# Kernel rows in two-bank PSUM tiles, and one exponent fewer: a change to an S4 layer's forward and backward pass

## The chip, the cores and the metric

The kernel runs on one core of a Trainium2 chip. The metric is the device time of one execution in microseconds, from start to end; lower is better. Each core has a matrix engine (PE, with its weight loads shown apart as PEld), a vector engine (DVE), a scalar engine (ACT), a general engine (POOL) and a queue engine (SP) that issues most DMA transfers. Each engine works through its own instruction stream in order and waits on semaphores for the others. Matrix products are written to PSUM, which has eight banks of 512 fp32 columns in each of 128 partitions; only DVE and ACT can copy them out to SBUF, the working memory.

## The reference

The computation is one layer, forward and backward. The forward part, cut to what matters:

```python
xn = _layernorm(x)                                   # x: [1, 2048, 512]
dt = exp(log_dt)[:, None]
P  = exp((dt * (A_re + 1j*A_im))[:, :, None] * arange(L)[None, None, :])   # [512, 128, 2048]
K  = einsum("dn,dnl,dn->dl", Cc, P, dt * Bc).real    # convolution kernel, 512 x 2048
s  = irfft(rfft(xn, padded) * rfft(K, padded))[:L] + xn * Dskip
g  = silu(silu(xn @ w1) @ w2)
out = x + s * g
```

The kernel returns `out` and the gradients of a scalar product with `grad_out` with respect to x, A, B, C (real and imaginary parts), log_dt, Dskip, w1 and w2. The sequence has L = 2048 rows, 512 channels, 128 states per channel, and a feed-forward width of 1792.

## The kernel before

**Kernel rows.** The powers of exp(dt*A) are never formed for all 2048 exponents. Exponent l is split into a sum of an exponent of a table E and one of a table Y. `E_EXP` has 21 entries (256 to 2048 in steps of 256, 0 to 7, and five sums of these), and `Y_EXP` has ten (8 to 56 in steps of 8, and 64, 128, 192). The 512 channels are worked in four blocks `b` of 128, each in two halves `h` of 64. For each half

- `gen_magnitudes` has written, in setup, the magnitudes exp(Re * e) of all 31 exponents (one ACT exponential each, L516) to the DRAM tensor `Md`;
- `gen_phases` (stream P) forms the phases, 16 and then 15 exponents at a time: a DVE product (L572), a DVE shift (L575) and an ACT sine (L579);
- `gen_powers` (stream Q) loads the half's magnitudes (L593) into a part of the tile `ds`, multiplies phase by magnitude on DVE (L607) into E, Y and H, stores E (`Ed`, L609), forms the remaining Y by six DVE products (L618 to L622), and stores Y (`Yd`, L624). E and the magnitudes have one buffer, so the load of the next half waits for the last power product of the half before, and it stands on SP's queue behind the store of Yd;
- `gen_kernel_rows` (stream R) multiplies E by C*B into W (two DVE products for eight channel groups, L642), then forms the kernel rows by PE: for each channel group `q` four matmuls of 84 columns accumulate (L648). Four groups fill a tile `ps_k` of 336 columns, which is copied to `ds` (the part called Xr) in another order of its axes. The tile's tag `pt` has one buffer of one bank. After both halves, rows are selected and summed from Xr by `put` (L660, `ps_e`, `ps_f`) and go by DMA to `Kb` in time order.

**Convolutions.** `gen_conv_x` (X), `gen_conv_fwd` (C) and, in the backward pass, `gen_conv_bwd_fwd` (D) and `gen_conv_bwd` (B) do Fourier transforms by matmuls. Every step fills a PSUM tile of tag `pc` (two buffers of two banks) and copies it to SBUF (1024 columns, or 2048 of bf16). **Feed-forward**: J turns rows, F is the forward product (tag `pf`, three buffers of one bank), and later come A, x, d, w, v, t for its gradients. N, Y, V, T, S, Z give the gradients of A, B, C and dt; `gen_ssm_fold` (N) sums kernel gradients per exponent of E.

**Order.** All engines run under a manual schedule. Each stream is a Python generator that issues a few instructions between two `yield`s. `PLAN` is a string of seven parts with one character per step, and `play` takes one step of the stream named by each. Part 0 is setup, part 1 the kernel rows and forward convolutions, part 2 the gate, part 3 the backward convolutions and feed-forward, parts 4 to 6 the parameter gradients. So PLAN alone sets each engine's and each queue's order. `SLOTS` names, allocation by allocation, which buffer of a tag is taken. `WAYS` has one string per stream: letter by letter, whether its next PSUM copy is made by ACT (`A`, L114) or DVE (`D`, L115).

The functions that the change touches are printed here with the line numbers of the profile.

## Time and profile before

| | us |
|---|---|
| median of 3 runs | 576.76 |
| the three runs | 576.76, 574.21, 577.73 |
| profiled execution, its own time | 574.64 |
| span from first to last instruction in it | 572.9 |
| mean granted TensorE clock | 0.987 of full speed |

The profiled execution is 2.1 us below the median; 1.7 us of its time lie outside the span. The page of the profile gives each engine's busy time as a share of the span, groups of instructions (line, engine, operation, output and input, shapes, count, busy us, mean ns of one, the idle time of the engine before them and who ended it), and the queues of DMA. A view by stretches gives busy time for windows of the span. A releaser is the instruction whose semaphore ended a wait. A busy PE isn't a PE at its peak, since matmuls are pipelined. The span starts at the first instruction, and each stage of PLAN follows the one before with some overlap: setup to about 42 us, rows and forward convolutions to about 206, the gate to about 245, the backward convolutions to about 366, and parameter and weight gradients to the end.

### The profile page before, as it was taken

How to read it: one execution, taken by the hardware profiler on the slowest of the kernel's cores; microseconds unless marked ns; L12 is line 12 of the kernel's file. 1: busy time of each engine (PE TensorE's matmuls, PEld its weight loads, DVE VectorE, ACT ScalarE, POOL GpSimd, SP SyncE). 2: the span in 40 equal slices, each digit the busy share in tenths (PEclk: the TensorE clock that was granted, in tenths of full speed). 3: DMA queues.
4: the chain of work that ended last, by engine and by line, in shares of the span. 5: the costliest groups of instructions: out<-in, count | busy, mean ns of one | idle time of the engine just before them, and what ended most of it. 6: DMA issues, size and time to landing. Idle time of an engine off the chain costs nothing.

```text
span 572.9 us, 14534 instructions
## 1 busy us (share of the span) xinstructions
PE 526.5 (92%) x6008; PEld 394.0 (69%) x6008; DVE 524.7 (92%) x818; ACT 448.1 (78%) x559; POOL 78.3 (14%) x164
## 2 busy tenths in 40 slices
PE   0589998999998999999999999999999999999993
PEld 0346776586767676876677766777678797776772
DVE  7999989999999779999998899969999999993994
ACT  6989998999999859998998977573575786662662
POOL 4251102010100011000010000000000030332221
PEclk9799998999999999999999999999999999999998
DMA  8978798899979989878989789898999998998982
GB/s 229 310 298 229 206 289 255 294 265 244 336 230 252 318 269 345 273 265 242 355 240 287 236 264 295 228 216 159 297 229 208 244 275 212 217 239 261 174 223 101
DMA packets 156644, 144.75 MB, mean 253 GB/s; under 512 B 83489, under 2 KB 132897, under 8 KB 153505
## 3 DMA queue, kind: packets, MB, share of 16 engines
q1 hardware_dynamic: 146816, 121.00, 78.7%
q0 software_dynamic: 6640, 19.67, 10.1%
q10 hardware_dynamic: 3120, 3.15, 1.8%
q8 instruction: 47, 0.77, 0.6%
q14 instruction: 21, 0.16, 0.1%
HBM read 62.91 MB, written 59.38 MB: 213 GB/s over the span
## 4 chain that ended last, share of the span: by engine, by line
PE 38%; DVE 31%; issue 10%; DMA 8%; ACT 6%; POOL 3%; SPq 2%; ACTq 0%; POOLq 0%; DVEq 0%
PE ps_da L1165 7%; PE ps_dx L1189 6%; PE ps_i L449 4%; PE ps_i L462 3%; DMA ds<-Md 3%; PE ps_o L777 3%; PE pt_t L136 2%; PE ps_s L432 2%; DVE Tq L1034 2%; DVE ds L607 2%; PE ps_w L1228 2%; DVE Tp L1034 2%; PE ps_s L404 2%; DMA out_dram<-gout 2%; DVE Tp L1038 2%
## 5 line engine op out<-in xcount | busy, mean ns | idle before, releaser
L114 ACT CAST dA<-ps_s 128x1024 bf16<-128x1024 f32 x86 | 86.6, 1035 | 7.5 <-PE ps_s L404 5.2
L760 PE MATMUL ps_h<-XT,W 128*128 128x256 bf16 x448 | 59.5, 283 | 11.0 <-ACT hT L114 6.6
L114 ACT CAST Vb<-ps_v 128x672 bf16<-128x672 f32 x55 | 39.1, 734 | 28.0 <-PE ps_v L1017 24.5
L760 PEld LDWEIGHTS <-W 128*128 128x128 bf16 x448 | 43.8, 102 | 19.7 <-issue 12.1
L1165 PE MATMUL ps_da<-doT,W 128*128 128x256 bf16 x448 | 56.9, 273 | 0.0
L1257 PE MATMUL ps_w<-dh_tok,xn 128*128 128x256 bf16 x448 | 52.4, 273 | 0.0
L777 PE MATMUL ps_o<-W,aT 128*128 128x512 bf16 x224 | 51.2, 379 | 0.2
L1189 PE MATMUL ps_dx<-W,dhT 128*128 128x512 bf16 x224 | 50.9, 379 | 0.0
L1228 PE MATMUL ps_w<-YD,a_tok 128*128 128x512 bf16 x224 | 50.6, 379 | 0.0
L114 ACT CAST dB<-ps_i 128x1024 bf16<-128x1024 f32 x42 | 41.9, 1031 | 10.6 <-PE ps_i L449 10.4
L1257 PEld LDWEIGHTS <-xn 128*128 128x128 bf16 x448 | 43.0, 98 | 5.7 <-issue 0.4
L1165 PEld LDWEIGHTS <-W 128*128 128x128 bf16 x448 | 41.2, 98 | 6.9 <-issue 1.2
L1168 DVE TENSOR_TENSOR dhT<-ps_da,dhT 128x512 bf16<-128x512 f32 x56 | 37.5, 685 | 7.0 <-PE ps_da L1165 6.7
L777 PEld LDWEIGHTS <-aT 128*128 128x128 bf16 x224 | 21.1, 98 | 25.1 <-ACT aT L768 1.2
L1189 PEld LDWEIGHTS <-dhT 128*128 128x128 bf16 x224 | 21.2, 98 | 24.8 <-issue 1.6
L1228 PEld LDWEIGHTS <-a_tok 128*128 128x128 bf16 x224 | 21.6, 98 | 23.2 <-ACT a_tok L1219 0.2
L114 ACT CAST o<-ps_w 128x256 bf16<-128x256 f32 (+1 forms) x37 | 16.2, 442 | 21.4 <-PE ps_w L1257 10.3
L579 ACT ACTIVATE sn<-V 128x2048 bf16<-128x2048 int16 (+1 forms) x16 | 30.2, 1890 | 0.9 <-DVE ds L607 0.5
L1219 ACT ACTIVATE a_tok<-pt_t 128x1024 bf16<-128x1024 bf16 x28 | 28.7, 1039 | 2.2 <-PE pt_t L136 2.1
L477 DVE TENSOR_TENSOR sp_in<-sp_in,dA 128x2048 bf16<-128x2048 bf16 x24 | 29.3, 1223 | 0.6
L475 DVE TENSOR_TENSOR cm<-sp_in,dA 128x2048 bf16<-128x2048 bf16 x24 | 29.3, 1220 | 0.7
L449 PE MATMUL ps_i<-I,sp_in 64*128 64x128 bf16 x768 | 27.6, 217 | 2.1 <-ACT dB L114 1.1
(240 smaller groups left out, 1244.6 us busy)
## 6 DMA issues: line engine op xcount, KB each, us to landing
Yd<-YD SPq DMA_DIRECT2D x8, 1024.0 KB, 5.2
sp_in<-Ud SPq DMA_DIRECT2D x8, 1024.0 KB, 8.2
h_in<-Hd SPq DMA_DIRECT2D x14, 512.0 KB, 5.1
Ed<-ds SPq DMA_DIRECT2D x8, 672.0 KB, 6.3
Eb<-Ed SPq DMA_DIRECT2D x8, 672.0 KB, 5.6
Hd<-hT POOLq DMA_DIRECT2D x8, 512.0 KB, 7.2
Ud<-dA SPq DMA_DIRECT2D x8, 512.0 KB, 7.2
KXd<-dA SPq DMA_DIRECT2D x4, 1024.0 KB, 5.3
```

Source lines behind the costliest of these rows:

```text
L114: return self.nc.scalar.copy(out=out, in_=in_)
L449: nc.tensor.matmul(out=ps[:, z, g], lhsT=Y[zs, c, g0 + g, :], rhs=k.I2[zs, c].rearrange("p c m -> p (c m)"), start=(c == 0), stop=(c == 1))
L475: TT(out=t2[:], in0=b[:, :, gs], in1=a[:, 1:2, gs].to_broadcast([P, 2, n, P]), op=ALU.mult)
L477: TT(out=b[:, :, gs], in0=b[:, :, gs], in1=a[:, 0:1, gs].to_broadcast([P, 2, n, P]), op=ALU.mult)
L579: nc.scalar.activation(out=sn[:, 0:n], in_=low, func=ACT.Sin, scale=-2 * PI_LO / 2.0 ** PB)
L760: nc.tensor.matmul(out=ps[:, j], lhsT=k.W1[:, dk, ft * P:ft * P + P], rhs=XTv[:, :, dk, :], start=(dk == 0), stop=(dk == DK - 1))
L777: nc.tensor.matmul(out=ps[:], lhsT=aT[:, ft, t * P:t * P + P], rhs=k.W2[:, ft, :], start=(ft == 0), stop=(ft == FT - 1))
L1165: nc.tensor.matmul(out=ps[:, j], lhsT=k.W2[:, ft, dk * P:dk * P + P], rhs=dTv[:, :, dk, :], start=(dk == 0), stop=(dk == DK - 1))
L1168: nc.vector.tensor_tensor(out=dh[:, i0:i0 + 2, :], in0=ps[:], in1=dh[:, i0:i0 + 2, :], op=ALU.mult)
L1189: nc.tensor.matmul(out=ps[:], lhsT=dhs[ft // 8][:, ft % 8, t * P:t * P + P], rhs=k.W1[:, :, ft * P:ft * P + P], start=(ft == 0), stop=(ft ...
L1228: nc.tensor.matmul(out=ps[:], lhsT=at[:, t, :], rhs=k.do[:, t, :], start=(t == 0), stop=(t == k.T - 1))
L1257: nc.tensor.matmul(out=ps[:], lhsT=k.xn[:, t, dk * P:dk * P + P], rhs=dh[:, t].rearrange("p j n -> p (j n)"), start=(t == 0), stop=(t == k ...
```

## The change

- **Two-bank tiles for the rows.** `ps_k` moves from tag `pt` (one buffer, one bank) to tag `pc` (two buffers, two banks, shared with the transforms), has eight channel groups of 128 columns each, of which 84 are used, and is copied once for eight groups: 16 copies of 672 columns instead of 32 of 336. The 32 matmuls are issued in two steps of 16 before the copy.
- **Exponent zero once.** The exponent 0 is put first in `E_EXP`, and phases, magnitudes and power products run over the 30 others (`X_EXP`). Its power, 1 + 0i, is written once into E by two memsets in `gen_first_powers`. Phases come 15 and 15 at a time instead of 16 and 15, and `Md` has 30 entries. E's entries are numbered anew, and the later users of the rows and the fold follow.
- **Order, slots and ways are made anew** for the whole kernel, in all seven parts of PLAN.

```diff
 PLAN = """
-221p32551512p5566073777171165553766767777J767774J6376777pF6767703076767884p6J7677777707F6067FJF86F46673F5F743FF776646FF6
...
+221325p5325515566767571677777766647701JJ70p7775076F6377766F76pF774770J786877J3F773177F06p6676643643F86853376F174F76FFFF6
...
-WAYS = """J=DAADADAA;
-F=AAADAAAAADADDAAAADADAAAAAAAAAAAAAAAAAAAAAAADADDAAAAAAAAADDDADAAADADDDAAA;
+WAYS = """J=DDADADAA;
+F=ADAAAAAAADDAAADAAADAAAAAAAAAAADAAAAAAAAAAAAADDAAAAADAADADDDAAADADDDAAAA;
...
-R=AAAAAAAAAAAAAAAAAAADAADDDAADAAAAAADAADAAAAAAAAAA;
-C=DDDAAAAAAAAAAAAAAAAADDAAAAAAAADAAAAAADAADAADDAADADADDDADAAAAAAAA;
+R=AAAAAAAAAAADAADAAADAAADAAAAAAAAA;
+C=ADDADAAAAAAAAAAAAAAADDAAAAAAAADDAAAAADAAAAADADAAADADDDADAAAAAAAA;
...
-D=AAAADDAAAAAAAAADAAAAAADAAADAAAAAAADAADA;
-d=DDAADAAA;
-B=AAAAAAAAAAAAAADAAAAAAAAAAAAAAAAAAAAAAADAAADAAADAAAAAAAADADA;
-x=AADAAAADADAA;
-V=DAADADDADAAAADAADDAAAAAAAAAAAAAAAAADAAAAAAAAAAAAAAAAAAAAAAAAAAAA;
-Y=AADDDAAA;
-w=AADAAAAAAADAAA;
-v=DAADAAAAAAADAAAAAAAAAAAAAAAA"""
+D=AAAADDAAAAAAAAADAADAAAAAAAAAADAADAAAAAA;
+d=DDADDAAD;
+B=AAAAAAAAAAADAADAADAAAAAAAAAAAAAADAADAAAADAADADAAAAAAAADAA;
+x=AADAADADDADA;
+V=DAAADAAAAAAAAAAAAADADAAADAAAAAAAAAAAAAAAAAAAAAAAAAAAAAAAAAAAAAAA;
+Y=DAAAAAAA;
+w=DADADDAAAAAAAA;
+v=AAADAADAAAADADAAAAAAAAAAAAAA"""
...
-E_EXP = [256 * i for i in range(1, 9)] + list(range(8)) + [258, 260, 262, 516, 772]
+E_EXP = list(range(8)) + [256 * i for i in range(1, 9)] + [258, 260, 262, 516, 772]
 Y_EXP = [8 * j for j in range(1, 8)] + [64, 128, 192]
 NE = len(E_EXP)
+X_EXP = E_EXP[1:] + Y_EXP
+NX = len(X_EXP)
...
-    for i, e in enumerate(E_EXP + Y_EXP):
+    for i, e in enumerate(X_EXP):
         nc.scalar.activation(out=mag[:, :, i], in_=lamr[:].rearrange("p (b d) -> p b d", b=8), func=ACT.Exp, scale=float(e))
...
     for Y in k.Y:
         k.nc.vector.memset(Y[:, 0, :, 0, :], 1.0)
         k.nc.vector.memset(Y[:, 1, :, 0, :], 0.0)
+    E = k.ds[:].rearrange("p t d -> p (t d)")[:, 0:2688].rearrange("p (c q e a) -> p c q e a", c=2, q=16, a=4)
+    k.nc.vector.memset(E[:, 0, :, 0, :], 1.0)
+    k.nc.vector.memset(E[:, 1, :, 0, :], 0.0)
     yield
...
-    for (x0, n) in ((0, 16), (16, 15)):
+    for (x0, n) in ((0, 15), (15, 15)):
...
-            parts = ((E[:, :, :, 0:16, :], 0, 16),)
+            parts = ((E[:, :, :, 1:16, :], 0, 15),)
...
+            ps = k.pc.tile([P, 8, 128], F32, name="ps_k", tag="pc")
             for u in range(2):
-                ps = k.pt.tile([P, 4, 84], F32, name="ps_k", tag="pt")
-                for q in range(4):
+                for q in range(4 * u, 4 * u + 4):
                     for m in range(4):
-                        nc.tensor.matmul(out=ps[:, q], lhsT=Y[:, m % 2, q0 + 4 * u + q].rearrange("p j a -> p (j a)"),
-                                         rhs=W[:, m, 4 * u + q].rearrange("p e a -> p (e a)"), start=(m == 0), stop=(m == 3))
+                        nc.tensor.matmul(out=ps[:, q, 0:84], lhsT=Y[:, m % 2, q0 + q].rearrange("p j a -> p (j a)"),
+                                         rhs=W[:, m, q].rearrange("p e a -> p (e a)"), start=(m == 0), stop=(m == 3))
                 yield
-                qq = 16 * h + q0 + 4 * u
-                k.ev(Xr[:, :, :, qq:qq + 4], ps[:].rearrange("p q (e a) -> p a e q", a=4))
-                yield
+            k.ev(Xr[:, :, :, 16 * h + q0:16 * h + q0 + 8], ps[:, :, 0:84].rearrange("p q (e a) -> p a e q", a=4))
+            yield
...
```

More of the change, by code (lines that the diff above doesn't have):

```diff
@@ L200, in setup_tiles @@
     t.prod = t.prod0, t.prod1
-    new("mag_all", [8, NE + len(Y_EXP), 64], BF16)
+    new("mag_all", [8, NX, 64], BF16)
     new("x_sb", [k.T, D], BF16)
@@ L587, in gen_powers @@
     TT = nc.vector.tensor_tensor
-    NX = NE + len(Y_EXP)
     qe = lambda ap: ap.rearrange("p e c (q a) -> p e c q a", a=4)
@@ L663, in gen_kernel_rows @@
     for a in range(4):
-        nc.tensor.matmul(out=ps[:, 0], lhsT=k.SEL[:, 0, a], rhs=Xr[:, a, 8:16, :], start=(a == 0), stop=(a == 3))
-    for i, n, t0, t1, terms in ((1, 1, 0, 2, ((0, 0),)), (1, 1, 2, 3, ((0, 16),)), (1, 1, 3, 6, ((0, 17),)), (1, 1, 6, 7, ((0, 18),)), (1, 1, 7, 8, ((1, 0), (2, 1))),
-                                (2, 2, 0, 3, ((0, 1),)), (2, 2, 3, 6, ((0, 19),)), (2, 2, 6, 8, ((1, 1), (2, 2)))):
+        nc.tensor.matmul(out=ps[:, 0], lhsT=k.SEL[:, 0, a], rhs=Xr[:, a, 0:8, :], start=(a == 0), stop=(a == 3))
+    for i, n, t0, t1, terms in ((1, 1, 0, 2, ((0, 8),)), (1, 1, 2, 3, ((0, 16),)), (1, 1, 3, 6, ((0, 17),)), (1, 1, 6, 7, ((0, 18),)), (1, 1, 7, 8, ((1, 8), (2, 9))),
+                                (2, 2, 0, 3, ((0, 9),)), (2, 2, 3, 6, ((0, 19),)), (2, 2, 6, 8, ((1, 9), (2, 10)))):
         put(ps[:, i:i + n, t0:t1], terms)
```

84 lines of the change are left out of this document (43 added, 41 removed).

## The prediction

> **What bounds the kernel now.** I read the page's engine rows first, then its slices, then a table of busy time by stretch, then the groups by line and shape, the waits and the timeline.
>
> ```profile
> PE 526.5 (92%) x6008; PEld 394.0 (69%) x6008; DVE 524.7 (92%) x818; ACT 448.1 (78%) x559; POOL 78.3 (14%) x164
> PEclk9799998999999999999999999999999999999998
> 0.00:42.00 42.00, 19.53 (x122) 12.35 (x123) 38.39 (x100) 35.41 (x53) 17.14 (x67) 0.92 0.94 278
> 42.00:206.00 164.00, 154.51 (x1921) 116.51 (x1920) 156.82 (x202) 152.32 (x178) 18.50 (x22) 0.99 0.90 268
> 206.00:245.00 39.00, 38.01 (x532) 29.57 (x529) 35.07 (x45) 34.84 (x38) 4.87 (x8) 1.00 0.85 290
> 245.00:366.00 121.00, 120.25 (x1472) 87.53 (x1471) 114.51 (x153) 103.22 (x107) 6.47 (x12) 1.00 0.86 271
> 366.00:410.00 44.00, 42.69 (x431) 30.80 (x430) 37.74 (x52) 21.75 (x24) 0.00 (x0) 1.00 0.98 208
> 410.00:515.00 105.00, 103.36 (x1154) 82.07 (x1152) 101.26 (x166) 73.28 (x116) 18.30 (x33) 1.00 1.07 236
> 515.00:573.00 58.00, 48.16 (x388) 35.21 (x385) 40.91 (x106) 27.27 (x46) 13.00 (x23) 0.96 0.74 190
> ```
>
> The columns of the stretches are: length, then busy us of PE, PEld, DVE, ACT and POOL, then granted clock, DMA share and GB/s. The first stretch is the setup, the second the stage of the change (kernel rows, forward convolutions, most of the feed-forward), the third the gate, and so on in the order of the plan. From 245 to 515 us PE is idle 0.75 + 1.31 + 1.64 = 3.7 us of 270: there PE bounds, and a copy saved elsewhere is worth nothing. Setup is led by DVE (38.4 of 42). From 42 to 245 us no engine is alone: PE is busy 192.5 of 203, DVE 191.9, ACT 187.2, so PE idles 10.5 us, DVE 11.1 and ACT 15.8. That is the stretch in which the change can earn, and 10.5 us is all there is to earn in it without shortening PE's own work.
>
> **The change part by part.** Its new form changes durations of these groups; counts of copies by engine come from the letters of the table WAYS (A is ACT, D is DVE), old against new.
>
> ```profile
> L516 ACT ACTIVATE mag_all<-lamr 128x512 bf16<-128x512 f32 x31 | 16.2, 613 | 1.1 <-DVE lamr L513 1.1
> L579 ACT ACTIVATE sn<-V 128x2048 bf16<-128x2048 int16 x8 | 15.6, 1946 | 0.7 <-DVE ds L607 0.5 <-DVE V L575 0.2
> L579 ACT ACTIVATE sn<-V 128x1920 bf16<-128x1920 int16 x8 | 14.7, 1835 | 0.2 <-DVE V L575 0.2
> L572 DVE TENSOR_TENSOR V<-tau,ecst 128x1024 int32<-128x1024 f32 x8 | 9.7, 1213 | 0.0
> L572 DVE TENSOR_TENSOR V<-tau,ecst 128x960 int32<-128x960 f32 x8 | 9.2, 1150 | 0.0
> L607 DVE TENSOR_TENSOR ds<-sn,ds 128x2048 bf16<-128x2048 bf16 x8 | 9.8, 1221 | 2.3 <-DMA ds<-Md 2.3
> L607 DVE TENSOR_TENSOR YD<-sn,ds 128x896 bf16<-128x896 bf16 x8 | 5.0, 620 | 0.0
> L114 ACT CAST ds<-ps_k 128x336 bf16<-128x336 f32 x28 | 12.8, 457 | 2.5 <-PE ps_k L648 2.4
> L115 DVE CAST ds<-ps_k 128x336 bf16<-128x336 f32 x4 | 2.0, 500 | 0.0
> L114 ACT CAST Vb<-ps_v 128x672 bf16<-128x672 f32 x55 | 39.1, 734 | 28.0 <-PE ps_v L1017 24.5 <-issue 2.6 <-ACT Gf L962 0.8
> L115 DVE CAST Vb<-ps_v 128x672 bf16<-128x672 f32 x9 | 7.6, 852 | 1.6 <-PE ps_v L1017 1.6
> L114 ACT CAST dA<-ps_s 128x1024 bf16<-128x1024 f32 x86 | 86.6, 1035 | 7.5 <-PE ps_s L404 5.2 <-PE ps_s L432 1.5 <-ACT hT L114 0.3
> L115 DVE CAST dA<-ps_s 128x1024 bf16<-128x1024 f32 x10 | 12.0, 1221 | 3.1 <-PE ps_s L432 2.4 <-PE ps_s L404 0.5
> L115 DVE COPY XT<-pt_t 128x1024 bf16<-128x1024 bf16 x3 | 2.0, 681 | 0.0
> L115 DVE CAST hT<-ps_h 128x512 bf16<-128x512 f32 x15 | 10.1, 679 | 0.2 <-PE ps_h L760 0.2
> L115 DVE CAST o<-ps_w 128x256 bf16<-128x256 f32 x3 | 1.2, 411 | 0.0
> L114 ACT CAST KE<-ps_f 128x384 bf16<-128x384 f32 x3 | 1.5, 495 | 0.0
> L561 DVE MEMSET YD<- x2: 85/85/85, 44.5 to 44.6; 128x32 uint32 x2
> L648 PE MATMUL ps_k<-W,YD 128*128 128x84 bf16 x512 | 25.5, 203 | 3.0 <-DVE YD L622 2.6 <-ACT ds L114 0.4
> ```
>
> Instructions of one engine overlap: the 31 exponentials last 613 ns each but fill 16.2 us, or 523 ns each, so one that follows another takes about 0.09 us less of the queue than its duration. I price every copy net of that.
>
> *Wider copies of the kernel rows.* 32 copies of 336 columns become 16 of 672. No 672-column copy of ps_k exists yet; the nearest row is Vb<-ps_v, also 672 columns out of two banks, 734 ns on ACT and 852 on DVE. The new source is read with a step of 128 elements between channels where it was 84; the old strided copy (457 ns) lies on the line from the plain ones of other widths, so I take no penalty. ACT: 28 x (457 - 90) = 10.3 us becomes 14 x (734 - 90) = 9.0, saves 1.3. Were each copy paid at its full duration it would be 12.8 - 10.3 = 2.5; were the wide strided copy as slow as a 1024-column one (1035) it would lose 14 x 0.945 - 10.3 = 2.9. I stay near Vb. DVE: 4 x 0.41 becomes 2 x 0.76, saves 0.1. PE's matmuls stay 512 of the same shape (25.5 us): 0.
>
> *One exponent fewer.* The exponent 0 leaves the table. ACT: one exponential (0.52), and 8 sines of 2048 become 1920: 8 x 0.11 = 0.9. DVE: 8 phase products 1213 to 1150, 0.5; their shifts by the same ratio, 0.2; 8 power products 2048 to 1920, by the slope between 2048 (1221) and 896 (620), 8 x 0.067 = 0.5; two more memsets, 0.2 back. The transfers of Md shrink by a thirtieth; I cost that at nothing: a thirtieth of a landing of some 6 us (below) is 0.2 us. The renumbered exponents of the later sums and of the fold read the same widths: 0.
>
> *Copies that change engine* between 0 and 245 us: row R sends one 384-column copy from DVE to ACT, C one of 1024, and J one of XT from ACT to DVE. ACT +0.4 + 0.94 - 0.94 = +0.4; DVE -0.4 - 1.14 + 0.6 = -0.9.
>
> So ACT loses 1.3 + 0.5 + 0.9 - 0.4 = 2.3 us of work and DVE 0.1 + 1.0 + 0.9 = 2.0, each about a hundredth of the stretch. PE idles 10.5 us there, so it can take them: I book 2.1. The ends are 0 (PE is what is late, and the copies were hidden) and 2.9 lost to 3.7 gained by the widths above.
>
> *The order.* Three things can be read from it. First, setup:
>
> ```profile
> PE ps_h L760 <- ACT hT L114: 6.6, 1, 6.6
> 23.32 0.69 DVE L380 BATCH_NORM_STATS2 st<-x_sb 128x6 f32<-128x512 bf16 x1
> 24.78 0.56 ACT L114 CAST hT<-ps_h 128x512 bf16<-128x512 f32 x1
> 28.15 1.89 ACT L286 ACTIVATE TF<-prod 128x2048 bf16<-128x2048 int16 x1
> ```
>
> Now the first copy of hT stands behind all exponentials and PE waits 6.6 us for it. In the new order it stands behind 17 of 30, and XT 1 and hT 1 go to DVE. Behind that wait the next thing is late: the exponentials still end near 24.9, then the sine table TF, and hT 2 comes after TF. So PE does two or three fills earlier, not the rest. DVE, which leads setup, gets 0.6 us more (booked above). The loads of x for rows 8 to 15 fall behind more weight loads on SP's queue, but the layer norm asks for the first of them only at 23.32 us. I book 1.0 gained, between 0 and the 2.8 that PE idles from 40 to 60 us (17.2 of 20 busy).
>
> Second, the transfers of the magnitudes, each queued on SP behind the store of Yd, which waits for the last power product of the half before:
>
> ```profile
> DMA to landing us min/median/max: 3.1/6.2/8.8
> DVE ds L607 <- DMA ds<-Md: 2.3, 2, 1.8
> 74.53 8.81 DMA ds<-Md
> 151.59 8.31 DMA ds<-Md
> 80.00:100.00 20.00, 17.40 (x217) 14.34 (x216) 17.62 (x22) 17.36 (x24) 4.38 (x3) 0.91 0.91 254
> 87.60 5.49 SPq L680 DMA_DIRECT2D Kb<-KE  x8
> 180.00:200.00 20.00, 17.71 (x245) 13.32 (x241) 16.59 (x22) 16.54 (x20) 2.21 (x3) 1.00 1.02 302
> ```
>
> Between that product and the first use DVE has, adding up row means in the old order, 8.2 to 9.5 us of other work, and two of the seven loads so placed (8.81 and 8.31 us to landing) came late, 2.3 us in all. In the new order the cover is 7.9 to 9.9: the same chance of two late loads; if all eight took the longest time, 2 to 3 us more. The four groups of Kb transfers behind them keep their place: 0.
>
> Third, where copies move after 245 us. Row B sends 3 more copies of 1024 to DVE, d and x two more each of 1024 (bf16) and 512, D one fewer, V 4 fewer and Y 2 fewer. For 245 to 366 us that is 3 x 1.22 + 2 x 0.68 + 2 x 0.68 - 1.22 = 5.2 us more on DVE, which is idle 6.5 there; PE's fills are hidden behind PE, so 0, at worst 2 if the last of DVE's slack comes at the wrong times. The tail (PE 48.2 of 58) keeps its work: 0, within 1.5.
>
> *Sum*, against the profiled execution's own 574.64 us (span 572.9): 574.64 - 2.1 - 1.0 = 571.5. That execution is 2.1 below the median of 576.76, so on the median's level it is 573.6, a gain of 0.55%.
>
> *What a page says against it.* PE was idle 2.6 us between 80 and 100, and its granted clock in that window was 0.91 where windows with shorter idle have 1.00. The Trainium skill, page "TensorE: Matmul & The Clock Gate", section "A second HAM failure mode: psum-queue depth-cycling", says that a PE that idles briefly between groups, as it cycles through PSUM banks, falls back to the slow clock and pays to warm up again. The window agrees that idle and clock fall together; no run so far shows it from PSUM. It is the second rival's mechanism. The page "Perfetto Trace Analysis", section "Identifying the Most-Contended Engine", holds busy matmul time for a poor measure and would look at weight loads. By it PEld at 69% leaves DVE at 92% as the engine that counts, which is the third rival.
>
> **The rivals.** *One, the middle stretch closes up* (faster). The 42 to 206 us stretch idles 9.5 us of 164, the gate stretch 1.0 of 39. With two 2-bank buffers instead of one single-bank one PE need not wait for a copy between the two halves of a row group. If the stretch came down to the gate's rate, 4.2, and the clock from 0.99 to 1.00 (1.5 us of 154), it gains 6.8, with the 1.0 of setup 7.8: 569.0. Against it: waits of ps_k for its copy are 0.4 us in the whole trace.
>
> *Two, the two-bank buffers run short* (slower). The tag pc has two buffers; it served 100 fills in the stage (25 per channel block) and now serves 116, and a ps_k holds one for 32 matmuls (1.6 us) and a copy. Every transform's fill then waits for it, and ACT's and DVE's copies behind. The place is the alternation of R with X and C in the stretch 42 to 206. Price: a stretch like 80 to 100 cost 2.6 us idle and 0.09 x 20 = 1.8 of clock, 4.4 together. One such more cancels the gain; from two more, 8.8 - 3.1 = 5.7, it is slower by 1%: 582.5. For it: ps_s copies are already waited for, 5.2 + 1.5 us on ACT; against it, the old buffer pt is free for the rest.
>
> *Three, nothing comes of it*, since what counts is the work of DVE, the busiest engine beside PE, over the whole span. Beside the -2.0 up to 245 us and the +5.2 of the backward stage, V moves 4 copies off DVE (-3.4), Y two of 1024 (-1.4), and w and v move two of 512 and one of 256 onto it (+1.8): +0.2 in all, on 524.7. Its time is then 576.8 + 0.2 = 577.0, within 2. For it: DVE leads setup and the stretch of the change. Against it: after 245 us PE has no idle time and DVE has.
>
> **How the numbers follow.** A measurement of this kernel can tell about 1% (5.8 us) from no change. My sum has 0.46, its own range 570 to 577.5; rival one 0.21, rival two 0.15, rival three 0.18. Faster by over 1% (under 571.0): rival one and 0.04 of the sum's edge, 0.25. Slower by over 1% (over 582.5): rival two's upper half and more late loads, 0.15. The rest, 0.60, is within. The range 567.5 to 581.5 leaves out the far half of rival one, 0.08, and most of rival two, 0.11.
>
> **What would show it.** ps_k copies: 14 on ACT near 734 ns and 2 on DVE near 852; far above, the price of the wide copy was wrong. DVE and ACT busy 2 us less up to 245 us, and the stage's end (the last copy of S_b) 3 us earlier; if they are less busy and the end is not earlier, the order ate it. The 6.6 us wait of ps_h gone. New waits of ps_s or ps_i for ACT or DVE copies, with clock windows under 0.95 between 42 and 206, mean rival two. DVE near 120 of 121 in the backward stage with PE idle over 2 us there means that the copies moved to DVE do bind. I am wrong if 245 us on differs by more than 3 us.

## The result and the profile after

The changed kernel takes 580.81 us (median of 7 runs, 579.34 to 584.31). The kernel before took 576.75 beside it (7 runs, 574.21 to 577.73). The ratio is 1.0094, 95% interval [1.0068, 1.012]: just within the 1% called no change, but slower, where the prediction had 573.6. Its profiled execution took 584.31 us (span 582.5), the slowest of the seven, so the two profiles are 9.7 us apart where the medians are 4.1.

Busy time by stretch in the changed kernel (length, then PE, PEld, DVE, ACT, POOL, granted clock, DMA share, GB/s), for the stretches shown of before:

```profile
0.00:42.00 42.00, 19.55 (x122) 12.84 (x124) 37.83 (x101) 33.99 (x51) 18.80 (x68) 0.92 0.93 282
42.00:206.00 164.00, 153.07 (x1909) 114.91 (x1918) 156.14 (x201) 150.95 (x166) 16.14 (x21) 1.00 0.87 262
206.00:245.00 39.00, 36.84 (x525) 29.07 (x525) 32.89 (x43) 34.19 (x38) 4.87 (x8) 1.00 0.88 287
245.00:366.00 121.00, 120.04 (x1476) 87.37 (x1474) 117.16 (x157) 100.19 (x102) 6.48 (x12) 1.00 0.88 273
366.00:410.00 44.00, 39.96 (x400) 29.83 (x398) 30.36 (x43) 22.15 (x24) 0.00 (x0) 0.96 0.93 199
410.00:515.00 105.00, 102.95 (x1113) 80.13 (x1119) 102.68 (x166) 73.87 (x114) 16.98 (x31) 1.00 1.00 228
515.00:583.00 68.00, 56.44 (x454) 41.57 (x455) 44.81 (x115) 30.50 (x49) 14.28 (x25) 0.92 0.79 187
```

Up to 245 us DVE is busy 37.83 + 156.14 + 32.89 = 226.9 us against 230.3 before, and ACT 219.1 against 222.6. So the work that the change was to save is gone, 3.4 us on each; counted up to the end of the last copy S_b (239.2 us before, 240.1 after) it is 2.5 us on each. But PE has lost in two places: 366 to 410 us, where it is busy 39.96 instead of 42.69 at a clock of 0.96, and the end, which has 10 us more span for 8.3 us more busy PE at a lower clock.

The copies of the rows (by line and shape: busy, mean ns of one, idle before):

```profile
L116 ACT CAST ds<-ps_k 128x672 bf16<-128x672 f32 x14 | 10.2, 728 | 2.1 <-PE ps_k L652 2.0
L117 DVE CAST ds<-ps_k 128x672 bf16<-128x672 f32 x2 | 1.7, 848 | 0.0
```

They cost 728 and 848 ns; the prediction took 734 and 852. The waits (us in total, times, longest) show the old one of PE still there and, in the first three rows, three that have grown. Two of these in the kernel before, then the changed kernel:

```profile
ACT Gf L962 <- PE G L959: 3.1, 3, 1.7
DVE pd_l L1298 <- DMA out_dram<-gout: 2.8, 1, 2.8
```

```profile
ACT pd_l L1308 <- DVE m L1304: 11.7, 6, 5.8
ACT Gf L965 <- PE G L962: 11.5, 4, 9.4
DVE pd_l L1301 <- DMA dh_tok<-DHd: 10.0, 1, 10.0
PE ps_h L763 <- ACT hT L116: 6.3, 1, 6.3
```

To see where time is lost I compare the moments at which the same instruction starts. Two rows of the view by tile, of before and then of after (count, ns min/median/max, first and last start), read at their last number:

```profile
L114 ACT CAST S_b<-ps_i x6: 1012/1028/1137, 133.8 to 238.2; 128x1024 bf16<-128x1024 f32 x6
L648 PE MATMUL ps_k<-W,YD x512: 197/201/276, 60.2 to 199.3; 128*128 128x84 bf16 x171
```

```profile
L116 ACT CAST S_b<-ps_i x6: 1005/1016/1018, 134.7 to 239.1; 128x1024 bf16<-128x1024 f32 x6
L652 PE MATMUL ps_k<-W,YD x512: 197/201/213, 61.4 to 198.8; 128*128 128x84 bf16 x171
```

The same view of other tiles gives the rest, in us:

| start of | before | after | later by |
|---|---|---|---|
| last ps_k matmul | 199.3 | 198.8 | -0.5 |
| last copy of S_b (end of the gate's transforms) | 238.2 | 239.1 | 0.9 |
| last ps_dx matmul (fold) | 409.0 | 414.5 | 5.5 |
| last psS matmul | 513.4 | 518.3 | 4.9 |
| last gout on ACT | 521.0 | 525.8 | 4.8 |
| first sum of the layer norm (pd_l on DVE) | 529.7 | 537.8 | 8.1 |
| end of the span | 572.9 | 582.5 | 9.6 |

So in these two executions nothing is gained up to 239 us, 4.6 us are lost in the fold and 3.3 more between gout and the layer norm's first sum. From that sum to the end it is 43.2 us before and 44.7 after. The table tells where the time goes and not how much of it: the first execution is 2.1 us below its kernel's median and the second 3.5 above, so 5.6 of the 9.6 us are theirs alone.

In the diff shown above, some letters of WAYS are wrong in six lines. These are the right ones (the counts in the prediction were made from them):

```diff
-D=AAAADDAAAAAAAAADAAAAAADAAADAAAAAAADAAADA;
-B=AAAAAAAAAAAAAADAAAAAAAAAAAAAAAAAAAAAAADAAAADAAAAAAAADADA;
+F=ADAAAAAAADDAAADAAADAAAAAAAAAAADAAAAAAAAAAAAADDAAAAADAAADADDDAAADADDDAAAA;
+D=AAAADDAAAAAAAAADAAADAAAAAAAAAADAADAAAAAA;
+B=AAAAAAAAAAADAADAADAAAAAAAAAAAAAADAAADAAAAADAADAAAAAAADAA;
+V=DAAADAAAAAAAAAAAADADAAADAAAAAAAAAAAAAAAAAAAAAAAAAAAAAAAAAAAAAAAA;
```

### The profile page after: what moved, and what is told of

It is laid out like the page before. It is cut to its first block, busy times and chain, and to the rows that moved or that the text cites. A ratio compares the mean times of both kernels' runs of the same rounds, so it can differ in the third digit from the quotient of the medians.

```text
span 582.5 us, 14494 instructions
## 1 busy us (share of the span) xinstructions
PE 528.8 (91%) x5983; PEld 395.7 (68%) x6008; DVE 521.9 (90%) x820; ACT 445.8 (77%) x542; POOL 77.6 (13%) x164
## 4 chain that ended last, share of the span: by engine, by line
PE 45%; DMA 6%; DVE 4%; SPq 3%; issue 2%; ACT 1%; ACTq 0%; DVEq 0%
PE ps_w L1231 7%; PE ps_da L1168 7%; PE ps_w L1260 6%; PE ps_dx L1192 6%; DMA dh_tok<-DHd 4%; PE pt_t L138 3%; PE psS L1057 3%; PE ps_v L1020 3%; PE ps_i L451 2%; PE ps_i L464 2%; SPq L495 1%; PE ps_s L434 1%; PE ps_s L406 1%; DMA go_x<-in_A_u_dram 1%; PE pt_f L420 1%
## 5 line engine op out<-in xcount | busy, mean ns | idle before, releaser
L116 ACT CAST dA<-ps_s 128x1024 bf16<-128x1024 f32 x88 | 87.8, 1030 | 8.2 <-PE ps_s L434 3.8
L116 ACT CAST Vb<-ps_v 128x672 bf16<-128x672 f32 x59 | 41.7, 728 | 24.2 <-PE ps_v L1020 15.7
L1260 PE MATMUL ps_w<-dh_tok,xn 128*128 128x256 bf16 x448 | 55.0, 280 | 5.6 <-ACT o L116 3.3
L780 PE MATMUL ps_o<-W,aT 128*128 128x512 bf16 x212 | 49.3, 379 | 1.6 <-ACT aT L771 0.6
L1231 PE MATMUL ps_w<-YD,a_tok 128*128 128x512 bf16 x211 | 49.1, 379 | 0.7
L116 ACT CAST dB<-ps_i 128x1024 bf16<-128x1024 f32 x39 | 39.0, 1021 | 11.2 <-PE ps_i L451 11.2
L1020 PE MATMUL ps_v<-Gb,YT 128*128 128x168 bf16 x256 | 27.1, 238 | 5.6 <-ACT Vb L116 3.5
L584 ACT ACTIVATE sn<-V 128x1920 bf16<-128x1920 int16 x16 | 29.1, 1818 | 3.6 <-DVE ds L611 2.5
L116 ACT CAST o<-ps_w 128x256 bf16<-128x256 f32 (+1 forms) x34 | 14.7, 436 | 21.6 <-PE ps_w L1260 13.7
L1146 ACT ACTIVATE dhT<-dhT 128x2048 bf16<-128x2048 bf16 (+1 forms) x16 | 27.5, 1719 | 3.5 <-DMA dhT<-Hd 3.5
```

Source lines behind the costliest of these rows:

```text
L116: return self.nc.scalar.copy(out=out, in_=in_)
L584: nc.scalar.activation(out=sn[:, 0:n], in_=low, func=ACT.Sin, scale=-2 * PI_LO / 2.0 ** PB)
L780: nc.tensor.matmul(out=ps[:], lhsT=aT[:, ft, t * P:t * P + P], rhs=k.W2[:, ft, :], start=(ft == 0), stop=(ft == FT - 1))
L1020: nc.tensor.matmul(out=ps[:, u, 168 * c:168 * c + 168], lhsT=YT[:, c, q + u, :], rhs=Gb[:, q0 + q + u].rearrange("p w x -> p (w x)"), star ...
L1231: nc.tensor.matmul(out=ps[:], lhsT=at[:, t, :], rhs=k.do[:, t, :], start=(t == 0), stop=(t == k.T - 1))
L1260: nc.tensor.matmul(out=ps[:], lhsT=k.xn[:, t, dk * P:dk * P + P], rhs=dh[:, t].rearrange("p j n -> p (j n)"), start=(t == 0), stop=(t == k ...
```

## The experiments

Each was timed beside the kernel before. Ratios are to it, with their 95% intervals. In the diffs of PLAN only a few characters of a part stand.

**Which part of the order loses?** `e1_new_head_old_tail` is the changed kernel with parts 3 to 6 in the old order (five D steps, which the old order had in part 2, go ahead of part 3; SLOTS and WAYS follow). `e2_old_head_new_tail` is the kernel before with the new order there.

```diff
-/DDaDDDadDdDdsDEDAWEDdBoAAAA
-/NdYNxNxNNYVYNAAxVVAaYVAVYVV
-/VVVVhVVVThSttVtYTYSVThTtTVV
-/itgkvkivivhtkkvvwtkmkwgtmkk
+/DDDDDDdDasEddDWadDEoDAsBAAA
+/ANNNYAANYNYNxVAxVsaVVdAxAYV
+/hTthVtTtYtVYVtVTtVtVStTVVTh
+/itikhvkivvttkvkikvwvmtkvmwk
```

> The changed kernel, but parts 3 to 6 of PLAN, and the WAYS and SLOTS of their streams, as before (with five D steps put in front of part 3, since the new part 2 has five fewer). Theory one (the time is lost by the order made anew behind the gate: the first group of the fold at 394 to 402 us, where ACT waits 9.4 us for G, and the tail, where DVE waits 10.0 us before the first row sums): 573 to 577 us, and in the stretch after 366 us PE idle as before, 1.3 us in 44. Theory two (the wide row tiles in pc and the new order of the first three parts cost it, and the waits behind are what follows): 579 to 582 us, as the changed kernel.

> The kernel before, but parts 3 to 6 of PLAN, and the WAYS and SLOTS of their streams, as in the changed kernel (five D steps taken off the end of part 2). Theory one: 579 to 583 us, with both waits of the changed kernel, 4 us of PE idle more in the 44 us after 366 and a tail that is longer by 3 to 6 us. Theory two: 575 to 578 us, as before.

e1 took 576.66 us, ratio 0.9997 [0.9975, 1.0018]; e2 took 580.82, ratio 1.0075 [1.004, 1.0109]. So the whole loss is in parts 3 to 6 (3.9 us by e2's median), and rows, exponent and the new order of parts 0 to 2 together are worth between 1.4 us gained and 1.0 lost, by e1's interval.

**Can the local edits be had without the order?** `e3_new_order_old_rows` has the new order with the rows in one-bank tiles; `e4_old_order_wide_rows_one_exponent_less` has both edits in the old order, with a `pc` buffer taken at the first step of four where one is free.

```diff
-            ps = k.pc.tile([P, 8, 128], F32, name="ps_k", tag="pc")
             for u in range(2):
+                ps = k.pt.tile([P, 4, 84], F32, name="ps_k", tag="pt")
...
+                k.ev(Xr[:, :, :, qq:qq + 4], ps[:].rearrange("p q (e a) -> p a e q", a=4))
```

```diff
+            for step in (2, 3, 4, 5):
+                if step == start:
+                    ps = k.pc.tile([P, 8, 128], F32, name="ps_k", tag="pc")
+                    fill(ps, range(4))
+                if step == max(start, 4):
+                    fill(ps, range(4, 8))
...
```

> The changed kernel with its whole new order, but the kernel rows in one-bank tiles of four groups in tag pt and copied 336 columns at a time (the first copy is issued in the step of the second 16 matmuls). Theory one: 579 to 583 us, no more than 2 us from the changed kernel. Theory two, in the form that the shared two-bank buffers run short: 575 to 577 us, and the last row copy 2 to 4 us earlier than at 199 us.

> Both local edits (rows in two-bank tiles of pc with one copy of 672 columns, exponent zero written once) in the order of before: PLAN as before without one step of the exponentials, the steps of the rows at their old places, buffers of pc alternated anew. Theory one: 574 to 577 us, the gain of about 2 us that my sum gave for the two edits or a part of it. Theory two: 579 us or more, with waits for pc tiles in the stretch 42 to 206 us.

e3 took 595.43 us, ratio 1.0334 [1.0272, 1.0396]; e4 took 596.9, ratio 1.0351 [1.0306, 1.0395]. Both are far from what was expected. The waits of e3, then of e4:

```profile
PE ps_k L652 <- ACT ds L116: 16.6, 15, 2.9
ACT ds L116 <- PE ps_k L652: 12.1, 14, 2.3
```

```profile
ACT dA L117 <- PE ps_s L407: 16.5, 17, 2.2
```

In e3 a one-bank tile must be copied before the second half of the row group can be filled, and the new order leaves no other work between them. In e4 the transforms wait: between 42 and 206 us PE's fills of ps_s wait 8.7 us for ACT's copies of dA and 3.0 us for its copies of the rows, where e1 has 0.9 and 0.3. Two `pc` buffers serve 16 more tiles there, in an order not made for that. Both results are about an order that doesn't fit its tiles, so neither measures what an edit is worth. They do show that the edit and the order can't be had apart here. A shortage of `pc`, the prediction's second rival, can be dear: both edits in the old order cost 20 us (596.9 beside 576.93).

**The fold or the end?** `e6_new_tail_alone` is e1 with only parts 5 and 6 new; `e7_old_tail_alone` is the changed kernel with only those two old.

```diff
-/hTthVtTtYtVYVtVTtVtVStTVVTh
-/itikhvkivvttkvkikvwvmtkvmwk
+/hVVVhttVtYTYSVThTtTVVTtVwTY
+/itgkvkivivhtkkvvwtkmkwgtmkk
```

```diff
-/VVVVhVVVThSttVtYTYSVThTtTVV
-/itgkvkivivhtkkvvwtkmkwgtmkk
+/VVVVTShTthVtTtYtVYVtVTtVtVS
+/itikhvkivvttkvkikvwvmtkvmwk
```

> Kernel rows, exponent and parts 0 to 4 as in e1_new_head_old_tail (576.7 us); only the last two parts, from the 128 V fills to the layer norm's sums, are in the new order. Theory A (the loss has two places, the fold at 376 to 420 us and the end): part of the 4 us comes back, 578 to 579.5, with the wait of the last layer norm sums for late stores (10 us) still there and that of Gf for G (11 us in the new order) back at 3. Theory B (the end alone loses): as the changed kernel, 580 to 581.5. Theory C (the fold alone loses, the late stores are only its echo): 576 to 577.5 and no 10 us wait of pd_l.

> The mirror of the run before: the changed kernel with its last two parts in the old order, so the new backward stage and the new fold stand alone. Theory A: 578 to 579.5, with the 11 us wait of Gf for G and a wait of pd_l of about 3. Theory B: 576 to 577.5. Theory C: 580 to 581.5.

e6 took 578.26 us, ratio 1.0004 [0.9976, 1.0032]; e7 took 580.75, ratio 1.0052 [1.0027, 1.0077]. By its ratio e7 says that parts 3 and 4 (backward stage and fold) lose about half a per cent by themselves; its median lies where theory C put it, and e6's where theory A did. e6 alone can't be told from no loss, though its profile has a 9.2 us wait of pd_l for late stores. The two don't add up to 1.0094 by their midpoints; what is left lies within the intervals, or in an end that loses more when the fold before it is late. So these two runs don't decide.

**The fold's cause.** In the changed kernel's timeline (start, us, engine, line, operation) G's second eight matmuls stand 6 us behind the first fourteen, and behind a ps_v fill that waits for a load; ACT stands for 9.4 us at Gf, and V's fills have nothing to work on:

```profile
394.26 1.19 PE L962 MATMUL G<-GE,FO 128*128 128x32 bf16 x14
...
400.41 0.39 PE L1020 MATMUL ps_v<-Gb,YT 128*128 128x168 bf16 x3 [0.99 <-DMA YT<-Yd]
...
401.51 0.38 PE L962 MATMUL G<-GE,FO 128*128 128x32 bf16 x8
401.97 1.86 ACT L965 CAST Gf<-G 128x2048 bf16<-128x2048 f32 x1 [9.41 <-PE G L962]
```

`e10_second_half_of_G_next` moves three steps of part 4:

```diff
-VNAxTTAxVANNAVTTN
+VNNNNAxTTAxVAAVTT
```

> The changed kernel with one thing moved in part 4: the second eight matmuls of block 1's G and the two copies Gf follow the first matmuls at once, not behind three ps_da, two ps_dx and a ps_v fill (15 us). Theory F (the fold's loss is this one misplaced step: V's fills have no Gf, PE stands 2.6 us at 396 to 406 us and its clock falls): the 9.4 us wait of Gf goes, PE is busy 9.5 of 10 there, the last ps_dx comes 2 to 4 us earlier against S_b, and the time is 577 to 579 against 580.8. Rival: the backward stage before it (copies moved to DVE) used the filler up, another wait takes its place: 580 to 581.5.

It took 577.59 us, ratio 1.0025 [1.0005, 1.0046]. In its timeline the 22 matmuls are one group at 393.92. Busy time by stretch, of the changed kernel and then of e10:

```profile
396.00:406.00 10.00, 6.39 (x57) 4.29 (x55) 6.26 (x9) 3.74 (x4) 0.00 (x0) 0.96 1.05 271
406.00:416.00 10.00, 10.00 (x77) 6.53 (x75) 7.12 (x12) 2.28 (x4) 0.00 (x0) 0.87 0.66 144
```

```profile
396.00:406.00 10.00, 10.00 (x84) 6.41 (x83) 9.36 (x14) 4.78 (x6) 0.00 (x0) 1.00 1.09 284
406.00:416.00 10.00, 8.47 (x97) 6.28 (x95) 9.55 (x14) 6.22 (x9) 0.00 (x0) 1.00 1.04 279
```

PE is busy 18.5 of 20 instead of 16.4, at full clock instead of 0.96 and 0.87, and the last ps_dx follows the last S_b by 408.7 - 239.4 = 169.3 us instead of 175.4. So this misplaced step is the fold's loss, 3.2 us by the medians. The 6.1 us of the two profiles is too much: the same distance is 172.2 us in e1 and 174.9 in e11 (below), which have the same fold.

**The end's cause.** In the changed kernel DVE is done with g_acc at 527.7 and starts the first sum at 537.75, although its pd_l was asked for at 514.7. The tile `m` that the sum writes lies where gout and g_acc lay, so the sum waits until their stores have landed. In the kernel before the same wait is 2.8 us, and its releaser is a store of gout. POOL's and DVE's rows of the timeline:

```profile
526.21 3.19 POOL L1119 DMA_DIRECT2D out_dram<-gout  x6 [0.19 <-issue]
527.47 0.27 DVE L1125 TENSOR_TENSOR g_acc<-pd,dt 1x128 bf16<-1x128 f32 x1
529.39 0.51 POOL L1127 DMA_DIRECT2D out_dram<-g_acc  x1
537.75 0.69 DVE L1301 SCALAR_TENSOR_TENSOR pd_l<-pd_l,ds 128x512 bf16<-128x512 bf16 x1 [10.01 <-DMA dh_tok<-DHd]
```

The releaser that is named, a load of dh_tok, doesn't explain the wait: the sum doesn't read dh_tok. The stores of gout land later than before: the six issued between 515 and 545 us took 9.4 us from issue to landing (median), against 5.4 in the kernel before. Why they are slower is not shown. The next three kernels give `m` memory of its own: `e12_changed_ln_sums_own_memory` in the changed kernel, `e11_ln_sums_own_memory` in e1, and `e13_both` in the changed kernel together with e10's move.

```diff
     k.jk = fw.tile([P, D], BF16, name="jk")
+    k.lnm = fw.tile([P, 2, 2, 4], F32, name="lnm")
...
-            m = lw.tile([P, 2, 4], F32, name="m", tag="m", bufs=2)
+            m = k.lnm[:, c % 2]
```

> e1_new_head_old_tail (576.7 us) with the small tile m of the layer norm's sums in memory of its own (64 bytes a partition in the pool fw), not where g_acc and gout lay, so that the first sum need not wait until the last stores of gout and g_acc have landed. Theory T (the end is set by the chain of DVE products that starts there, 43 us from its start to the end in every run): the wait of 3.6 us goes and the time is 572 to 574. Rival (the loads of pd_l and Gt behind the same landing, or PE's w1 matmuls, set the end): 575.5 to 577.

> The changed kernel with the same tile m in its own memory. Theory T: the 10 us wait of the first sum goes; the first three blocks of sums take 9 to 12 us, by which time the fourth has landed: 572 to 576 against 580.8. Rival (late stores hold the fourth load of pd_l, and the wait only moves there): 578 to 580.

> The changed kernel with both edits, G's second half next and m in its own memory. If the two losses are separate the gains add: some 3 + 6 us, 570 to 574 against 580.8. If the late stores are the echo of the late fold, the second gain is smaller by what the first gives: 573 to 577.

e11 took 575.33 us, ratio 0.9978 [0.9955, 1.0], between its two expectations; e12 575.17, ratio 0.9979 [0.9955, 1.0003]; e13 570.98, ratio 0.9906 [0.987, 0.9942]. The timeline of e12 at the same place:

```profile
527.36 3.20 POOL L1119 DMA_DIRECT2D out_dram<-gout  x6 [0.19 <-issue]
528.62 0.27 DVE L1125 TENSOR_TENSOR g_acc<-pd,dt 1x128 bf16<-1x128 f32 x1
528.81 0.67 DVE L1301 SCALAR_TENSOR_TENSOR pd_l<-pd_l,ds 128x512 bf16<-128x512 bf16 x1
530.55 0.51 POOL L1127 DMA_DIRECT2D out_dram<-g_acc  x1
```

The sum follows g_acc at once, while the stores are still on their way. The wait is gone and 5.6 us with it (by the medians). The two gains add: 3.2 + 5.6 = 8.8 by the medians, 9.8 measured. e13 is the changed kernel with its two losses mended, and is faster than before.

`e17_before_ln_sums_own_memory` gives the kernel before the same tile and nothing else.

> The kernel before with the tile m in its own memory and nothing else. e11 gained 1.3 us by it on the old tail, so 575 to 576 against 576.7; the rest of e13's gain (570.98) would then come from the new order and the local edits. If it reaches 571 to 573, e13's gain is this edit's alone.

It took 574.35 us, ratio 0.9935 [0.9909, 0.9961], more than expected. So by the midpoints two thirds of e13's gain over the kernel before belong to this edit, which has nothing to do with the change. The rest, 0.9906 against 0.9935, has overlapping intervals, so e13 doesn't show that the mended change is worth anything over the mended kernel before. e18 and e19 (below), which are e13 with one more exchange of steps each, have 0.9865 [0.9831, 0.9899] and 0.9864 [0.9825, 0.9903], both clear of e17's interval: that points to a gain of some 0.7%. It doesn't lie ahead of S_b, which starts at 238.4 us in e17 and at 239.2 in e18.

**The first 245 us.** The work fell and the end of the stretch did not come earlier. `e8_magnitudes_asked_earlier` asks, in e1, for the next half's magnitudes behind Ed, not behind Yd, and puts the one such load that stood behind eight transfers of Kb ahead of them:

```diff
-    nc.sync.dma_start(tab[:, 5376:5376 + 64 * NX], k.Md[2 * b + h])
+    if b == h == 0:
+        nc.sync.dma_start(tab[:, 5376:5376 + 64 * NX], k.Md[0])
...
     nc.sync.dma_start(k.Ed[b, h], tab[:, 0:2688])
+    if 2 * b + h < 7:
+        nc.sync.dma_start(tab[:, 5376:5376 + 64 * NX], k.Md[2 * b + h + 1])
```

> e1_new_head_old_tail with the load of the next half's magnitudes issued behind the store Ed, not behind the store Yd three products later, and the one such step that stood behind eight loads of Kb put ahead of them. Theory H (the work taken off DVE and ACT in the first 245 us was given back at waits like the 2.9 us that DVE stood for this load at 100 us): those waits go, 573 to 575.5 against 576.7. Rival K (those engines had room there and the stretch is paced by PE and the order's other waits): 576 to 577.5 with the waits of ds gone.

It took 577.02 us, ratio 0.9995 [0.9966, 1.0024], with S_b at 240.9: no gain. The waits of ds are gone, and between 100 and 110 us PE is busy 9.72 us where e1 has 7.72. But the transfers of Kb, now behind the magnitudes, come late: they take 4.8 us to land (median of eight; 2.5 in e1), PE stands 3.0 us for them (0.3 in e1), and between 90 and 100 us it is busy 6.77 us, where e1 has 8.12. So the run exchanged one wait for another, and what the wait for the magnitudes alone is worth stays open. `e9_an_eighth_of_each_row_copy` shortened the row copies:

```diff
-            k.ev(Xr[:, :, :, 16 * h + q0:16 * h + q0 + 8], ps[:, :, 0:84].rearrange("p q (e a) -> p a e q", a=4))
+            k.ev(Xr[:, :, :, 16 * h + q0:16 * h + q0 + 1], ps[:, 0:1, 0:84].rearrange("p q (e a) -> p a e q", a=4))
```

> e1_new_head_old_tail with each kernel row copy writing one of its eight channel groups (84 columns instead of 672; the other rows stay at the zero of one memset on POOL), so ACT loses another 14 x 0.45 = 6 us of work in 42 to 206 us. If ACT's work is worth its time there, as the sum of the prediction took it: 570 to 572. If it is hidden behind PE and the order: 575.5 to 577. Between them, 573 to 575, it is worth a part.

It was slower, 581.63 us, ratio 1.0068 [1.0041, 1.0096]. The added memset is the likely cause: POOL does it from 40.7 to 43.1 us, and between 42 and 50 us, ahead of the first row copy, PE was busy 5.99 us at a clock of 0.57, where e1 has 7.26 at 1.00. It says nothing about ACT. The next three repeat the question on e13, each taking work off one engine, and each without a memset: `e14_less_DVE_work`, `e15_less_ACT_work` and `e16_less_PE_work`.

```diff
+        n = 8 if b > 0 and c == 1 else 16
-        TT(out=m1[:], in0=lo(x[0]), in1=hi(x[1]), op=ALU.mult)
+        TT(out=m1[:, 0:n], in0=lo(x[0])[:, 0:n], in1=hi(x[1])[:, 0:n], op=ALU.mult)
...
```

```diff
+            n = 1 if b > 0 else 8
+            k.ev(Xr[:, :, :, 16 * h + q0:16 * h + q0 + n], ps[:, 0:n, 0:84].rearrange("p q (e a) -> p a e q", a=4))
```

```diff
-                    for m in range(4):
+                    ms = (0, 3) if b > 0 else (0, 1, 2, 3)
+                    for m in ms:
```

> e13_both (570.98 us; the last copy of S_b at 239.1 us, at 239.1 to 240.9 in the eight profiles with the new order ahead of it) with the imaginary powers of blocks 1 to 3 made for eight of sixteen channel groups only, the rest left from the block before: 18 DVE products of 0.95 us become about half, 8 us less DVE work before 190 us. If DVE's work is worth its time there, as the sum of the prediction took it: 563 to 566, S_b near 232. If DVE waits for the order as much as it works: 569 to 571.5, S_b at 238 to 240. Between: worth a part.

> e13_both with the row copies of blocks 1 to 3 writing one channel group of eight (84 columns; the rest left from block 0), without the memset on POOL that disturbed e9: about 11 copies shorter by 0.45 us, 5 us less ACT work before 200 us. If ACT's work is worth its time there: 565 to 567, S_b near 234. If it is hidden: 569.5 to 572, S_b at 238.5 to 240.5.

> e13_both with two of the four products in each kernel row of blocks 1 to 3 left out: 192 of the 512 ps_k matmuls fewer, 9.6 us less PE work before 200 us. If PE paces the stretch 42 to 206 us (busy 153.5 of 164): 562 to 565, S_b near 230. If DVE paces it: 569 to 571.5. Between: no one engine paces it.

| | work taken off | time, us | ratio | last S_b |
|---|---|---|---|---|
| e13 | - | 570.98 | 0.9906 [0.987, 0.9942] | 239.1 |
| e14 | DVE 7.2 | 568.87 | 0.9848 [0.9799, 0.9898] | 239.4 |
| e15 | ACT 2 | 570.9 | 0.9893 [0.9827, 0.9959] | 245.5 |
| e16 | PE 7.2 | 569.45 | 0.9862 [0.9805, 0.9919] | 237.2 |

e14's work is 18 products that fell from 951 to 551 ns; in the groups by shape, for one of the three lines:

```profile
L623 DVE TENSOR_TENSOR m<-YD,ds 128x1536 bf16<-128x1536 bf16 x10 | 9.5, 953 | 0.1
L623 DVE TENSOR_TENSOR m<-YD,ds 128x768 bf16<-128x768 bf16 x6 | 3.3, 553 | 0.1
```

The copies of e15 fell only by 0.2 us each, so that run tests little (its S_b is that of an execution of 576.48 us; the other three took 569.5 to 571.2):

```profile
L116 ACT CAST ds<-ps_k 128x84 bf16<-128x84 f32 x10 | 5.3, 530 | 4.5 <-PE ps_k L652 4.3
```

All four intervals overlap. Taking 7.2 us off DVE left S_b where it was, and 7.2 us off PE brought it 1.9 us forward; the last ps_k, which starts at 199.0 us in e13, came at 197.6 in e14 and 196.9 in e16. The profile of e14 is of the slowest of its four executions (571.5 us) and that of e16 of the fastest (567.72). By the medians 7.2 us of work are worth 2.1 and 1.5 us, neither clear of the noise. So neither DVE's work nor PE's is worth its full time in this stretch; a part is not excluded. Where the rest goes, into waits of the order for one another, is argued and not shown.

**Two waits of the new order there.** `e18_hT_ahead_of_sine_table` puts, in e13, three steps of stream 4 (the sine table TF among them) behind the copies of hT and the first Silu. `e19_last_rows_copies` exchanges, in e13, the last transform's fills with the matmuls of ps_e.

```diff
-F06p6676643643F86853376F174F76FFFF6
+F06p66766363F86853376F17F76F444FFF6
```

```diff
-RRCCCCCR
+RCCCCCRR
```

> e13_both (570.98 us) with the sine table TF in the setup put behind the hT copies 2 and 3 and the first Silu, not ahead of them, so that PE's 6.3 us wait for hT at 23.7 to 30 us becomes some 3. If that wait is worth time, as the prediction's 1.0 for the setup took it: 569 to 570.2. If PE's fills there are not late (the layer norm on DVE sets the end of the setup, 41 us): 570.5 to 572 with the wait shorter.

> e13_both with one pair of steps exchanged at the end of part 1: the last transform's third and fourth fill and their dA copies ahead of the 64 matmuls of ps_e and ps_f, as they were before, so that the copy KE does not stand behind a dA copy that itself waits 2.1 us for PE. If that wait is the 1.4 us by which the stretch from the last ps_k to the last S_b grew (38.9 before, 40.3 us in every profile of the new order): the stretch 39 to 39.6, the time 569.5 to 570.5. If PE paces it: 40 to 40.5, 570.5 to 572.

e18 took 569.82 us, ratio 0.9865 [0.9831, 0.9899]. PE's wait split in two (its waits between 20 and 50 us):

```profile
PE ps_h L763 <- ACT hT L116: 2.9, 1, 2.9
PE pt_t L138 <- ACT hT L116: 2.6, 1, 2.6
```

The wait fell by little, from 6.3 to 2.9 + 2.6 = 5.5 us, so the run tests less than it was meant to. S_b starts at 239.2, as in e13 (239.1). The time lies between the two expectations, and its interval overlaps e13's. e19 took 570.63 us, ratio 0.9864 [0.9825, 0.9903]. What it was to mend is seen in ACT's timeline of before and of after:

```profile
200.10 1.01 ACT L114 CAST dA<-ps_s 128x1024 bf16<-128x1024 f32 x1
202.61 1.01 ACT L114 CAST KE<-ps_e 128x1024 bf16<-128x1024 f32 x1 [1.49 <-DMA Yd<-YD]
```

```profile
199.64 1.02 ACT L116 CAST dA<-ps_s 128x1024 bf16<-128x1024 f32 x1
202.78 1.01 ACT L116 CAST dA<-ps_s 128x1024 bf16<-128x1024 f32 x1 [2.12 <-PE ps_s L434]
203.69 1.02 ACT L116 CAST KE<-ps_e 128x1024 bf16<-128x1024 f32 x1
```

A dA copy that waits for PE stands ahead of KE, and KE starts 1.1 us later. In e19 the stretch from the last ps_k to the last S_b fell from 40.3 to 39.6 us, as the wait's theory has it, but the last ps_k itself came 2 us later (201.0) in that execution, ahead of which nothing was changed, and the time is no better than e13's. That this wait is the 1.4 us stays open.

## Why the prediction was wrong

*Wider copies.* The price was right: 728 and 848 ns against 734 and 852. *One exponent fewer.* The work fell as said. Together with the copies that changed engine DVE and ACT lost 2.5 us each up to the last copy of S_b, against 2.0 and 2.3 forecast. (The ends given to this step don't add up: with the widths at 2.5 gained or 2.9 lost ACT's sum is 3.5 gained or 1.9 lost. Nothing hangs on it.)

*"PE idles 10.5 us there, so it can take them: I book 2.1"* was the first step to fail. The prediction itself had named the sign: less busy and the end not earlier means that the order ate it. S_b starts 0.9 us later (238.2 before; 237.8 and 238.4 in e2 and e17, which also have the old order up to there). e1, with all of this and the old rest, has 0.9997, and its interval, at most 1.4 us gained, leaves out the 3.1 booked for this step and the setup together. e14 and e16 point to the reason: 7.2 us off DVE and off PE moved S_b by 0 and 1.9 us, so idle time of PE is not simply filled by work taken off another engine. That the 10.5 us are waits of one step for another in a fixed order, where a shorter copy makes the next wait longer, fits e8 and e14; it is not shown for the copies of the rows.

*"I book 1.0" for the setup* failed too. The wait for hT is 6.3 us after, 6.6 before. ACT's first copy of hT did come 6 us earlier (18.80 us, before 24.78), but the wait moved to its next one, which stands behind the sine table at 29.36 us; the exponentials ended at 26.1 us, not near 24.9. PE is busy 19.55 us up to 42 us, before 19.53. The prediction had seen that hT 2 comes after TF and booked a gain nevertheless.

*The order after 245 us.* That copies moved to DVE stay hidden behind PE in the backward stage was right: DVE is busy 117.16 of 121 and PE 120.04. *"The tail (PE 48.2 of 58) keeps its work: 0, within 1.5"* is the step that failed by most, and the fold (366 to 410 us) had no term at all. The work was kept (from 245 us to the end DVE is busy 294.4 us before and 295.0 after, ACT 225.5 and 226.7), but I priced an order by the work in it, and did not read parts 4 to 6 of the new PLAN step by step, as I did for the magnitudes. Two places there decide the result: G's second half behind three ps_da, two ps_dx and a ps_v (e10: 3.2 us), and late stores under the tile of the layer norm's first sum (e12: 5.6 us, of which the kernel before would also have gained 3.0: 577.35 beside e17, and 574.35). "I am wrong if 245 us on differs by more than 3 us" is what happened: from S_b to the end it is 343.4 us in the profile after and 334.7 before, and by the medians e2, which has the old order up to there, loses 3.9 us.

*The rivals.* The first (569.0) did not come: 42 to 206 us did not close up. The second (582.5) has nearly the time, by chance, but not the mechanism: the stretch has a clock of 1.00, and ACT waits 3.8 + 3.6 us for ps_s, little more than before. The page of the Trainium skill that stood behind it, "TensorE: Matmul & The Clock Gate", section "A second HAM failure mode: psum-queue depth-cycling", ties an oscillating clock to short idle times between groups of matmuls, as PE cycles through PSUM banks; here 16 more fills of `pc` left the clock at 1.00, and it fell to 0.96 and 0.87 where the fold left PE idle 3.6 of 10 us. The third (577.0, nothing comes of it) has the time that e1 measured for the head alone (576.66), but not the mechanism: it let DVE's total rise by 0.2 us and the time with it, and in the changed kernel that total fell by 2.8 us (524.7 to 521.9) while the time rose.

Not settled: why the first 245 us gave back what was saved in them; whether ACT's work is worth anything there (e15 took too little off); whether the KE copy is what makes the gate's stretch 1.4 us longer; how far a late fold makes the end's loss larger; why the stores of gout land later; and by how much the mended change beats the kernel before with the same tile moved (e13 570.98 and e17 574.35 us, with overlapping ratios; e18 and e19 lie clear of e17).

## What to carry to other kernels

Where a hand-written order is made anew, price it by its waits: follow, in each part, the few chains that feed the rest (here G to Gf to V, and stores to reused memory to the first sum) and see what each step stands behind on its engine; equal work says nothing. Where three engines are all busy above 90%, as from 42 to 206 us here, don't count the idle time of one as room that a shorter instruction on another will fill: take work off each engine in turn and look at where the stretch ends. A small tile that reuses memory of tiles still being stored can hold a whole chain: 64 bytes a partition were worth 3.0 us here before the change and 5.6 after it.

## What the runs showed of the hardware

A copy of 84 columns of ps_k on ACT took 530 ns, more than the 445 of 336 columns and not much less than the 718 of 672 (the first a mean of ten copies, the others medians). All are written with another order of axes; the eighth of a row is written one element at a time with a step, where the others write four or eight in a row. That this is the reason is not shown.

The Trainium skill, page "SBUF — State Buffer", section "Door 1: The DMA port swizzle", states that SBUF has lines of 16 bytes, that accesses one after another to the same line run at full bandwidth from two per line on, and that each access to a new line pays a penalty. By the layout of Xr all three forms above touch 84 lines, the copy of 84 columns once each and the others four and eight times. A price by lines alone would make the three alike, and one by lines and width would put 84 columns below 445; the 530 agrees with neither. It agrees with a loss where a line is touched only once, but no run here varies that alone.

At one gap the clock falls in some executions and not in others. The new order leaves PE idle some 2 us between 100 and 110 us in every profile (in e12 and e13 most of it in one wait, of 2.3 and 2.2 us). First e13, then e12, which issue the same instructions up to there:

```profile
100.00:110.00 10.00, 7.70 (x78) 4.12 (x76) 8.27 (x11) 7.82 (x8) 0.08 (x1) 1.00 0.91 331
```

```profile
100.00:110.00 10.00, 7.69 (x66) 4.17 (x64) 8.34 (x11) 6.80 (x7) 0.00 (x0) 0.83 0.90 331
```

With the same busy time the granted clock is 1.00 in one and 0.83 in the other. Of the ten profiles of kernels with this head and nothing left out (the changed kernel, e1, e6, e7, e10 to e13, e18, e19), four have 1.00 there and S_b at 239.1 to 239.4 us, six have 0.83 to 0.88 and S_b at 239.4 to 240.6. The Trainium skill, page "TensorE: Matmul & The Clock Gate", section "What's actually happening", says that the gate watches a window of 3.4 us that runs freely and doesn't start with the kernel. The rows agree with the length: one such window at half clock takes 1.7 us from ten, which is the 0.83, and in e12 the clock is 0.55 from 106 to 108 us, 0.59 from 108 to 110, and 1.00 in the 2 us ahead of them and behind them. The same section of the Trainium skill puts the fall after an idle window of about 3.4 us; here a gap of 2.3 us was enough, and the measurement decides. So a milestone in one profile is worth no more than about a microsecond. That the lower clock alone makes S_b later is not shown.
